# A recurrence-plus-MLP kernel: raw rooms without clears, first queries' values in quarter tiles, one masked copy on ScalarE, one reversal on VectorE

## The chip, the cores and the metric

The kernel runs on one core of one Trainium2 chip. The metric is the device time of one launch in microseconds, as the median of several runs. A core has five instruction queues that the text names as the profile does: PE (TensorE, with PEld for its weight loads), DVE (VectorE), ACT (ScalarE), POOL (GpSimd) and SP (SyncE, which here issues nearly all DMAs). Each executes its own instructions in the order in which the program issues them.

## The reference

Two blocks follow one another. The first is a gated linear recurrence for 4 batches and 8 heads over 768 tokens with head size 48; the second is a two-layer MLP with SiLU on the 3072 x 384 rows that come out.

```python
for t in range(S):                       # S = 768, D = 48
    cur = einsum('bhd,bhe->bhde', u[None] * kt, vt)
    y[:, :, t] = einsum('bhd,bhde->bhe', rt, state + cur)
    state = wt[:, :, :, None] * state + einsum('bhd,bhe->bhde', kt, vt)
x = y.transpose(0, 2, 1, 3).reshape(3072, 384)
h = x @ w_in                             # 384 x 2048
out = (h * (1 / (1 + exp(-h)))) @ w_out  # 2048 x 384
```

All inputs and outputs are 32-bit floats.

## The kernel before

**Units.** The work is cut into 12 units: 6 chunks of 128 tokens (`L`) times 2 pairs of batches (`NB = 2`). A unit holds 16 head-batches; 8 heads are 4 pairs `p` of an even and an odd head `e`, at partition rows 0 to 47 and 64 to 111. The second batch of a pair is kept in reversed token order.

**Scores by levels.** Within a unit the decayed products of queries and keys are made in 7 levels (`NL`), level `l` with blocks of `c = 2^l` tokens. `scores(i, l)` (L725) has PE make the products, and `keep_masked` (L719, its copy is L722) has DVE write them with a mask into the tile `score[128 keys, e, 8 (batch, pair), 128 queries]`. Levels in the tuple `COPIED` (L686) are written by plain ACT copies instead (L741). Level 6 writes only the second half of the queries (columns 64 to 127). The diagonal, the bonus with `u`, is written by `bonus_write` (L601, its copy L604), two DVE copies over the whole score. Between the levels POOL grows the keys (`grow_keys`, L645), ACT moves odd keys (L615) and DVE grows the queries (L627).

**Values.** `y(i, b)` (L873) multiplies values and scores for units 0 and 1: 4 pairs times 2 heads, each a matmul of 128 keys x 64 value columns against 128 queries (L879), and one ACT copy to `yt` (L883). `dense_x` (L911) packs the rows for the MLP, `up` makes 256 hidden columns with SiLU, `down` the second product.

**Loading.** Units 0 and 1 (`NTOK = 2`) load tokens of r, k, w into rooms `raw` (two slots, three rooms of 128 x 1024 each; a room's first 768 columns hold tokens and PE transposes them, reading up to 16 columns further). `twos` (L99) also names the 16 columns behind the tokens, and L264 clears them with one DVE memset for each of the six rooms, at the very start. Units from 2 on write the same rooms by blocks of 32 tokens (L123), which fill only 16 of 32 columns for half of the partitions; so `clear(i)` (L406, its ACT copy L401, 128 x 1536) zeroes these columns once for either slot. The values of batch 2 are loaded in one piece for units 0 and 1 (L138) and turned round by `reverse_v` (L410): a matmul with a mirror matrix (L414) and an ACT copy (L415). From unit 2 on they are loaded as four blocks of 32 rows (L143), and DVE turns each block (L417, a stream shuffle).

**Order.** The order is written out by hand with `do(...)`. For unit 0 the six levels run with other work between them (`others`), then y(0), `dense_x`, the first `up`; then the levels of unit 1 with `up` of unit 0; then y(1). Beside this the 16 pieces of the MLP's weights are rounded one after the other: `head_weight` (ACT L223, L225), `tail_weight` (ACT L231, writes the PSUM tile `p_w`), `join_weight` (DVE L242 and L243, reads it), `add_weight` (POOL L255). `p_w` has one buffer, and unit 0's diagonal stands in it before `bonus_write(0)` has read it. At the start DVE makes masks (L327 to L353) from counters that POOL writes into the score's memory; only then may POOL clear the score (L355), and after it POOL makes the first product of unit 0's bonus (L448).

Of the kernel before, what the change touches and what calls it, by code (L numbers as in the profile page):

```python
# [8 lines left out]
F32 = mybir.dt.float32  # L9
# [29 lines left out]
def kernel(  # L39
# [11 lines left out]
    nc = tc.nc  # L51

    B, H, S, D = r.shape
    DM, DF = moe_w_in.shape
    L = 128
    NL = 7
    NB = 2
    NP = H // 2
    PD = 64
# [7 lines left out]
    NSLOT = 2  # L67
    NTOK = 2
# [8 lines left out]
    ps = ctx.enter_context(tc.tile_pool(name="ps", bufs=1, space=bass.MemoryType.PSUM))  # L77
# [6 lines left out]
    def bank(name, *dims):  # L84

        have = banks[name][turns_of[name] % 2][:]
        turns_of[name] += 1
        steps, n = [], 1
        for d in dims[::-1]:
            steps.insert(0, [n, d])  # L90
            n *= d
        return bass.AP(tensor=have.tensor, offset=have.offset, ap=[have.ap[0], *steps])


    raw = const.tile([128, NSLOT, 3, NB, H, PD], F32, name="raw")
    WRK = {"w": 0, "r": 1, "k": 2}
    vt, vq, whole = {}, {}, {}

    def twos(room):  # L99

        flat = room.rearrange("p b h d -> p (b h d)")
        return flat[:, 0:H * 2 * D].rearrange("p (h s) -> p h s", h=H), flat[:, H * 2 * D:H * 2 * D + PD - D]

    def load_twos(to, src, i, queues):
        n, b0 = units[i]
# [4 lines left out]
    def load_tokens(i):  # L110
        for name, src in (("k", k), ("r", r), ("w", w)):
            load_twos(twos(raw[:, i % NSLOT, WRK[name]])[0], src, i, [nc.sync, nc.scalar if i == 0 else nc.sync])
# [13 lines left out]
    def load_values(i):  # L126
        n, b0 = units[i]
        t0 = n * L

        rooms = [pin.tile([128, H * D + PD - D], F32, name=name, bufs=2) for name in ("vt", "vq")]  # L130
        if n == 0:
            for room in rooms:
                nc.vector.memset(room[:, H * D:], 0.0)
        whole[i] = rooms
        vt[i], vq[i] = (room[:, 0:H * D].rearrange("p (h d) -> p h d", h=H) for room in rooms)
        nc.sync.dma_start(out=vt[i], in_=v[b0, :, t0:t0 + L, :].rearrange("h t d -> t h d"))
        if i < NTOK:
            nc.sync.dma_start(out=vq[i], in_=v[b0 + 1, :, t0:t0 + L, :].rearrange("h t d -> t h d"))  # L138
            return

        for g in range(4):
            t1 = t0 + L - (g + 1) * 32
            nc.sync.dma_start(out=vq[i][g * 32:(g + 1) * 32], in_=v[b0 + 1, :, t1:t1 + 32, :].rearrange("h t d -> t h d"))  # L143
# [114 lines left out]
    zero = const.tile([128, 1], F32, name="zero")  # L258
# [3 lines left out]
    for i in range(NTOK):  # L262
        for x in range(3):
            nc.vector.memset(twos(raw[:, i, x])[1], 0.0)  # L264
# [13 lines left out]
    load_tokens(1)  # L278
    load_weight(1)
    load_values(0)  # L280
    for i in due[-1][2:]:
        load_weight(i)
    load_values(1)

    ident = const.tile([128, 128], F32, name="ident")
# [5 lines left out]
    room = pt.tile([128, 4, DM // 2], F32, name="partial", bufs=1).rearrange("p x d -> p (x d)")  # L291
# [41 lines left out]
    NSC = 1  # L333
    score = const.tile([128, NSC, 2, Q, L], F32, name="score")
# [62 lines left out]
            to = t.rearrange("p (b q) (i s) -> p q b i s", b=NB, s=2)[:, :, :, :, s]  # L397
            nc.scalar.copy(out=to, in_=p_tr)

    def clear_all(room):  # L400
        nc.scalar.copy(out=room, in_=zero[:, :, None].to_broadcast(list(room.shape)))  # L401

    def clear_state():
        nc.gpsimd.memset(state, 0.0)

    def clear(i):  # L406

        clear_all(raw[:, i % NSLOT].rearrange("p x b h d -> p (x b h d)").rearrange("p (g d) -> p g d", d=32)[:, :, D - 32:32])

    def reverse_v(i):  # L410
        flat = vq[i].rearrange("p h d -> p (h d)")
        if i < NTOK:
            p_v = bank("p_m", H * D)
            nc.tensor.matmul(p_v, lhsT=mirror, rhs=flat, start=True, stop=True)  # L414
            nc.scalar.copy(out=flat, in_=p_v)  # L415
            return
        nc.vector.stream_shuffle(out=flat, in_=flat, mask=list(range(31, -1, -1)))  # L417
# [53 lines left out]
    at = 768  # L471
# [211 lines left out]

        return x % 2, x if x % 2 == 0 else (L >> l) - 1 - x

    COPIED = (0, 5, 0), (0, 6, 0), (1, 6, 0)  # L686

    def score_products(i, l, queries, sc):
        c, ni = 1 << l, L >> (l + 1)
# [35 lines left out]
    def scores(i, l, *between):  # L725
# [8 lines left out]
        def keep(e):  # L734
            if (i, l, e) in COPIED:

                for b in range(NB):
                    for x in range(ni):
                        first = 2 * x * c if b == 0 else L - (2 * x + 1) * c
                        rows, columns = slice(first, first + c), slice((2 * x + 1) * c, (2 * x + 2) * c)  # L740
                        nc.scalar.copy(out=score[rows, i % NSC, e, b * NP:(b + 1) * NP, columns],  # L741
                                       in_=sc[e][rows, b * NP:(b + 1) * NP, x * c:(x + 1) * c])
                return
            keep_masked(i, l, e, sc)
# [85 lines left out]
    p_yt, p_kv, yt = {}, {}, {}  # L830
# [28 lines left out]
    def y_values(i, e):  # L859
# [9 lines left out]
        for x in range(2):  # L869
            nc.scalar.copy(out=yt[i][PD * e:PD * e + D, x::2, :, :],  # L870
                           in_=p_yt[i, e][PD * x:PD * x + D].rearrange("p (q b) t -> p q b t", b=NB))

    def y(i, b):  # L873

        p_yt[i, b] = ps.tile([128, NP, L], F32, name="p_h", bufs=2) if i == 0 else bank("p_m", NP, L)
        for p in range(NP):
            for e in range(2):
                h = 2 * p + e
                nc.tensor.matmul(p_yt[i, b][PD * e:PD * e + PD, p, :], lhsT=whole[i][b][:, h * D:h * D + PD],  # L879
                                 rhs=score[:, i % NSC, e, b * NP + p, :], start=(p == 0), stop=(p == NP - 1))  # L880
        if b == 0:
            yt[i] = pt.tile([128, NP, NB, L], F32, name="yt", bufs=1)
        nc.scalar.copy(out=yt[i][:, :, b, :], in_=p_yt[i, b])  # L883
# [49 lines left out]
    def both(fn, i, *args):  # L933
        return [(fn, i, b, *args) for b in range(NB)]

    def block_loads(i, names="wkr"):
        return [(load_blocks, i, name, g) for name in names for g in range(4)]

    def mix(i):
# [43 lines left out]
        if i + 1 < len(units):  # L983
            loads.insert(len(loads) // 2, (load_values, i + 1))
# [109 lines left out]
    def do(*steps):  # L1094
        for fn, *args in steps:
            fn(*args)
# [7 lines left out]
    def back(fn, i, *args):  # L1104
# [6 lines left out]
       (make_dense,), (beat, 16))  # L1111

    blocks = block_loads(2)
    others = {1: [(clear, 0), (beat, 6)], 2: [(turn, 1, 0, "r"), (head_weight, 0), (beat, 2)],
              3: [(turn, 1, 1, "r"), (head_weight, 1), (beat, 2)], 4: [(turn, 1, 1, "w"), (reverse_v, 0)],
              5: [(bonus_spread, 0), (bonus_write, 0), (turn, 1, 0, "w")], 6: [*both(turn_in, 1, "k"), *blocks[0:4], (tail_weight, 0)]}
    for l in range(1, NL):
        do((scores, 0, l), *[(grow_keys, 0, l + 1)] * (l + 1 < NL), *others[l])

    do((bonus, 1, 0), (bonus, 1, 1), (bonus, 1, 2), *both(y, 0), (turn_apart, 0), (join_weight, 0), (add_weight,),  # L1120
       (product, 1, 0), (tail_weight, 1), (turn, 1, 0, "k"), (join_weight, 1), (dense_x, 0, 0), (turn, 1, 1, "k"),
       (dense_x, 0, 1), (grow_queries, 1, 0), (odd_ones, 1), (tail_weight, 2), (turn_k, 0), (head_weight, 2),
       (start_keys, 1, nc.gpsimd, True), (add_weight,), (up, 0, 0), (join_weight, 2), *blocks[4:8],
# [3 lines left out]


    others = {1: [(bonus_sum, 1, 0), (bonus_sum, 1, 1), (load_rk, 2), *blocks[8:12]], 2: [*both(update, 0)],
              3: [(bonus_spread, 1), (reverse_v, 1), (clear, 1), (load_values, 2)]}  # L1130

    def piece(i):

# [2 lines left out]
    for m in range(1, 4):  # L1136
        do((piece, m + 3), (scores, 1, m + 1), (grow_keys, 1, m + 2), (up, 0, m + 2), *others[m])
    do((head_weight, 8), (join_weight, 7), (scores, 1, 5), (grow_keys, 1, 6), (add_weight,), (tail_weight, 8), (up, 0, 6),
       (bonus_write, 1))

    do((scores, 1, NL - 1), (bonus, 2, 0), (bonus, 2, 1), (join_weight, 8), (add_weight,), (bonus_sum, 2, 0), (bonus, 2, 2), (up, 0, 7), *both(y, 1), (turn_apart, 1),
       (tail_weight, 9), (turn_k, 1), (dense_x, 1, 0), (head_weight, 9, [0]), (dense_x, 1, 1), (head_weight, 9, [1]),
       (join_weight, 9), (add_weight,), (tail_weight, 10), (head_weight, 10), *both(update, 1), (bonus_sum, 2, 1), (load_rk, 3), (up, 1, 0), *both(turn, 2, "w"))
    blocks = block_loads(3)

    others = {0: [(up, 1, 1), (down, 0, 0, 0), *both(turn, 2, "k"), (product, 2, 0), (product, 2, 1)],
              1: [(up, 1, 2), *both(turn, 2, "r"), *[(product, 2, l) for l in range(2, NL)], *blocks[0:3]],
              2: [(down, 0, 0, 1), (odd_ones, 2), (start_keys, 2, nc.gpsimd, True), (grow_queries, 2, 0), *blocks[3:6]],
              3: [(up, 1, 3), (start_keys, 2, nc.gpsimd, False), (reverse_v, 2), *blocks[6:9]], 4: [(level, 2, 1), (up, 1, 4), *blocks[9:12]],
              5: [(down, 0, 0, 2), (up, 1, 5), (weight_sums, 0)]}  # L1150
# [15 lines left out]
    for i in range(3, len(units)):  # L1166
# [4 lines left out]
        room = (1, 1, 0, 2, 1, 1, 1, 1, 1, 2, 2, 1, 1) if i < NPAIR else (2, 1, 2, 2, 1, 1, 1, 2, 1, 1, 1)  # L1171
# [37 lines left out]
```

## Time and profile before

| what | value |
|---|---|
| median of 4 runs | 601.8 us (601.66, 601.74, 601.85, 604.5) |
| the profiled execution | 600.91 us, of which the span of the core's instructions is 599.1 us |
| busy in the span | PE 590.7, PEld 529.9, DVE 417.9, POOL 361.4, ACT 232.9 us |
| granted TensorE clock | 1.0 in every slice |
| two ACT clears of raw rooms (L401) | 1.47 us each, at 16.06 and 60.01 |
| two reversals by mirror (L414, L415) | PE 0.9 us and ACT 0.48 us each, at 22.96 and 58.67 |
| y(0), y(1) (L879) | PE from 29.34 and from 66.57 to the next work at 31.71 and 68.47 |
| six memsets of 128 x 16 (L264) | 0.21 us together, 72 ns each, at 0.87 |

A line of the timeline has the start in us from the span's beginning, the length in us, engine, line, operation, output and input tiles, shapes and count; in brackets stands how long the engine was idle before it and what ended that. Several instructions of one kind in a row are merged to one line. In the chain of waits the work is followed back from the last instruction to what released it. An idle time of an engine that the end doesn't hang on costs nothing. The span's first 64 us are units 0 and 1, in which five queues wait for one another; behind them PE works nearly without a gap to the end.

### The profile page before, as it was taken

To read this page: it belongs to the slowest core of one execution; us is meant where nothing else is said; L and a number is where in the kernel's file an instruction comes from. 1 tells how busy PE (TensorE), PEld (TensorE's weight loads), DVE (VectorE), ACT (ScalarE), POOL (GpSimd) and SP (SyncE) were. 2 spreads that over 40 slices of the span, in tenths; PEclk is the share of its full clock that TensorE was granted. 3 is DMA by queue.
4 is the path that set the end of the run, shared out by engine and by line. 5 is a ranking of instruction groups with operands and counts; after the bars stand their busy time and mean duration, and the time that the engine had idled before them with its cause. 6 is when DMAs were issued, how large, how long until landed. Compare 5 with 4: busy or idle time off the path is not lost.

```text
span 599.1 us, 15465 instructions
## 1 busy us (share of the span) xinstructions
PE 590.7 (99%) x6142; PEld 529.9 (88%) x6142; DVE 417.9 (70%) x709; ACT 232.9 (39%) x516; POOL 361.4 (60%) x414
## 2 busy tenths in 40 slices
PE   8999999999999999999999999999999999999997
PEld 7787876799899899899899899889889889889997
DVE  7879788798696695596696696687587587542041
ACT  6788884431530530540450351361351251250110
POOL 6998778357678668378478478577467558500000
PEclk9999999999999999999999999999999999999999
DMA  9966693343542543642632743633553531101000
GB/s 225 294 143 188 135 309 47 55 79 49 130 63 57 110 65 54 135 62 51 139 59 52 139 61 55 133 59 53 109 84 51 121 55 27 36 2 28 27 1 26
DMA packets 203080, 53.45 MB, mean 89 GB/s; under 512 B 186752, under 2 KB 194816, under 8 KB 203008
## 3 DMA queue, kind: packets, MB, share of 16 engines
q1 hardware_dynamic: 201424, 51.88, 42.3%
q8 instruction: 48, 0.79, 0.6%
q10 hardware_dynamic: 1584, 0.59, 0.5%
q14 instruction: 24, 0.20, 0.1%
HBM read 43.21 MB, written 5.24 MB: 81 GB/s over the span
## 4 chain that ended last, share of the span: by engine, by line
PE 80%; DVE 6%; SPq 3%; DMA 3%; POOL 3%; issue 2%; ACT 2%; DVEq 0%; POOLq 0%; ACTq 0%
PE p_h L1001 35%; PE p_o L1067 31%; PE p_m L1023 3%; PE p_sc L704 2%; PE p_m L865 2%; SPq L123 2%; PE p_m L844 2%; PE p_m L704 2%; DVE score L722 1%; POOL tk L645 1%; DMA tokens_w<-in_w_dram 1%; PE p_sc L820 1%; DMA raw<-in_r_dram 1%; SPq L143 1%; PE p_sc L893 1%
## 5 line engine op out<-in xcount | busy, mean ns | idle before, releaser
L1001 PE MATMUL p_h<-xt,w_in_sb 128*128 128x256 f32 x1152 | 259.4, 382 | 0.8 <-POOL tk L669 0.7
L1001 PEld LDWEIGHTS p_h<-xt,w_in_sb 128*128 128x128 f32 x1152 | 215.7, 190 | 31.8 <-POOL tk L669 0.9
L1010 ACT ACTIVATE gt<-p_h 128x512 f32<-128x512 f32 x90 | 53.6, 596 | 175.1 <-PE p_h L1001 174.8
L645 POOL TENSOR_TENSOR tk<-tk,tw 128x256 f32<-128x256 f32 x128 | 94.3, 758 | 33.1 <-issue 20.8
L1067 PE MATMUL p_o<-own,temps 128*128 128x192 f32 x528 | 88.7, 327 | 0.4 <-DVE temps L1076 0.2
L1067 PEld LDWEIGHTS p_o<-own,temps 128*128 128x128 f32 x528 | 86.0, 190 | 1.3 <-DVE temps L1076 1.3
L507 POOL TENSOR_TENSOR ruk<-tokens_rk 128x768 f32<-128x768 f32 (+1 forms) x32 | 50.7, 1595 | 60.3 <-DMA tokens_rk<-in_k_dram 35.6
L1067 PE MATMUL p_o<-w_out_sb,gt 128*128 128x192 f32 x508 | 86.6, 327 | 0.0
L1067 PEld LDWEIGHTS p_o<-w_out_sb,gt 128*128 128x128 f32 x508 | 83.3, 190 | 1.0 <-DVE partial L1076 0.4
L1049 DVE TENSOR_TENSOR temps<-gt 128x256 f32<-128x256 f32 x84 | 58.0, 691 | 25.6 <-ACT gt L1010 25.4
L627 DVE TENSOR_TENSOR tr<-tr,tw 128x512 f32<-128x512 f32 x61 | 53.9, 883 | 17.8 <-PE p_m L704 14.1
L422 POOL TENSOR_TENSOR tw<-tw 128x256 f32<-128x256 f32 (+6 forms) x83 | 41.1, 495 | 35.1 <-DVE tw L374 31.2
L615 ACT COPY tk<-tk 128x256 f32<-128x256 f32 x52 | 21.0, 403 | 105.2 <-POOL tk L645 77.3
L722 DVE COPY_PREDICATED score<-mask,p_sc 128x512 f32<-128x512 int8 x42 | 31.2, 798 | 3.4 <-PE p_sc L704 3.2
L1049 DVE TENSOR_TENSOR temps<-temps,gt 128x256 f32<-128x256 f32 x43 | 30.7, 715 | 1.5
L1067 PE MATMUL p_o<-w_out_sb,temps 128*128 128x192 f32 x176 | 30.4, 326 | 0.0
L541 DVE TENSOR_REDUCE block_sums<-ruk 128x4 f32<-128x192 f32 (+1 forms) x48 | 24.2, 545 | 7.1 <-POOL ruk L507 7.1
L1067 PEld LDWEIGHTS p_o<-w_out_sb,temps 128*128 128x128 f32 x176 | 28.9, 190 | 0.0
L1076 DVE TENSOR_TENSOR partial<-p_o,partial 128x192 f32<-128x192 f32 x33 | 11.7, 355 | 24.4 <-PE p_o L1067 24.4
L870 ACT COPY yt<-p_m 48x512 f32<-48x512 f32 x40 | 23.2, 581 | 13.8 <-PE p_m L865 13.1
L1076 DVE TENSOR_TENSOR temps<-p_o,partial 128x192 f32<-128x192 f32 x22 | 7.8, 357 | 29.6 <-PE p_o L1067 23.3
L704 PEld LDWEIGHTS p_sc<-tr,tk 48*32 48x32 f32 (+1 forms) x1312 | 18.3, 119 | 11.2 <-issue 8.1
(188 smaller groups left out, 823.0 us busy)
## 6 DMA issues: line engine op xcount, KB each, us to landing
w_out_sb<-in_moe_w_in_dram SPq DMA_DIRECT2D x6, 768.0 KB, 7.7
w_out_sb<-in_moe_w_out_dram SPq DMA_DIRECT2D x4, 768.0 KB, 5.4
own<-in_moe_w_out_dram SPq DMA_DIRECT2D x4, 768.0 KB, 5.7
tokens_rk<-in_r_dram SPq DMA_DIRECT2D x8, 384.0 KB, 4.4
tokens_rk<-in_k_dram SPq DMA_DIRECT2D x8, 384.0 KB, 5.3
tokens_w<-in_w_dram SPq DMA_DIRECT2D x8, 384.0 KB, 6.3
xt<-yt SPq DMA_DIRECT2D x60, 48.0 KB, 1.9
raw<-in_w_dram SPq DMA_DIRECT2D x80, 32.0 KB, 2.1
```

The lines of the kernel that those rows point to most:

```text
L422: engine.tensor_tensor(out=up, in0=t[:, :, 0::2], in1=t[:, :, 1::2], op=ALU.mult)
L507: mul = lambda out, one, two: nc.gpsimd.tensor_tensor(out=out, in0=one, in1=two, op=ALU.mult)
L541: add = lambda out, have: nc.vector.tensor_reduce(out=out, in_=have, axis=mybir.AxisListType.X, op=ALU.add)
L627: nc.vector.tensor_tensor(out=odd, in0=odd, in1=tw[i][l][:, :, 0::2][:, :, :, None].to_broadcast([128, Q, L >> (l + 1), c]), op=ALU.mult)
L645: nc.gpsimd.tensor_tensor(out=out, in0=have, in1=odd_products(i, l, b, *blocks), op=ALU.mult)
L704: nc.tensor.matmul(to, lhsT=tk[i][rows, X[l % 2] + p, x * m:(x + 1) * m], rhs=have, start=True, stop=True)
L722: nc.vector.copy_predicated(out=dst, mask=masks[l][:, :, None].to_broadcast([128, NB, NP, ni, c]), data=sc[e].rearrange("p (b q) (i c) -> ...
L870: nc.scalar.copy(out=yt[i][PD * e:PD * e + D, x::2, :, :], in_=p_yt[i, e][PD * x:PD * x + D].rearrange("p (q b) t -> p q b t", b=NB))
L1001: nc.tensor.matmul(p_h[:, a, :], lhsT=w_in_sb[:, c, f * 128:(f + 1) * 128], rhs=xt[i][:, c, :], start=(c == 0), stop=(c == KC - 1))
L1010: nc.scalar.activation(out=gt[i, m], in_=p_h, func=AF.Silu)
L1049: nc.vector.tensor_tensor(out=out, in0=one, in1=two, op=op)
L1067: nc.tensor.matmul(p, lhsT=left(f), rhs=right[:, f, :], start=(f == 0), stop=(f == FH - 1))
```

## The change

Only the first two units are touched.

- `twos` names all 256 columns behind a room's tokens instead of 16, so the six memsets of L264 are 128 x 256. `clear` and `clear_all` are gone: what the blocks of units 2 and 3 leave unwritten holds old tokens, in rows that no result reads.
- Unit 1's batch-2 values are loaded in four blocks of 32 rows, as from unit 2 on, and turned by DVE. The step moves from beside level 4 of unit 1 to just ahead of `bonus_write(1)`. Unit 0 keeps the mirror.
- `COPIED` gains (0, 6, 1): the last level of unit 0 is written by ACT for the odd heads too.
- A new step `y_first` stands ahead of y(0) and y(1). For the first 64 queries only 64 keys count (rows 0 to 63 of batch 1, rows 64 to 127 of the reversed batch 2); it makes 16 matmuls of 64 x 64 weights against 64 queries, which use quarters of PE's array. `y` keeps the second 64 queries: 16 matmuls of 128 x 64 weights against 64 queries. Both PSUM tiles are taken at the beginning of `y_first`.

```diff
@@ twos
-        return flat[:, 0:H * 2 * D].rearrange(...), flat[:, H * 2 * D:H * 2 * D + PD - D]
+        return flat[:, 0:H * 2 * D].rearrange(...), flat[:, H * 2 * D:]
@@ load_values
-        if i < NTOK:
+        if i == 0:
             nc.sync.dma_start(out=vq[i], in_=v[b0 + 1, :, t0:t0 + L, :].rearrange("h t d -> t h d"))
             return
@@ clear_all and clear are taken out; reverse_v
-        if i < NTOK:
+        if i == 0:
@@
-    COPIED = (0, 5, 0), (0, 6, 0), (1, 6, 0)
+    COPIED = (0, 5, 0), (0, 6, 0), (0, 6, 1), (1, 6, 0)
@@
+    def y_first(i):
+
+        half = L // 2
+        for b in range(NB):
+            p_yt[i, b] = ps.tile([128, NP, L], F32, name="p_h", bufs=2) if i == 0 else bank("p_m", NP, L)
+        for p in range(NP):
+            for e in range(2):
+                for b in range(NB):
+                    at, rows = (2 * p + e) * D, slice(b * half, (b + 1) * half)
+                    nc.tensor.matmul(p_yt[i, b][PD * e:PD * e + PD, p, 0:half], lhsT=whole[i][b][rows, at:at + PD],
+                                     rhs=score[rows, i % NSC, e, b * NP + p, 0:half], start=(p == 0), stop=False)
+
     def y(i, b):
 
-        p_yt[i, b] = ps.tile([128, NP, L], F32, name="p_h", bufs=2) if i == 0 else bank("p_m", NP, L)
+        half = L // 2
         for p in range(NP):
             for e in range(2):
                 h = 2 * p + e
-                nc.tensor.matmul(p_yt[i, b][PD * e:PD * e + PD, p, :], lhsT=whole[i][b][:, h * D:h * D + PD],
-                                 rhs=score[:, i % NSC, e, b * NP + p, :], start=(p == 0), stop=(p == NP - 1))
+                nc.tensor.matmul(p_yt[i, b][PD * e:PD * e + PD, p, half:], lhsT=whole[i][b][:, h * D:h * D + PD],
+                                 rhs=score[:, i % NSC, e, b * NP + p, half:], start=False, stop=(p == NP - 1))
@@ the order
-    others = {1: [(clear, 0), (beat, 6)], ...
+    others = {1: [(beat, 6)], ...
-    do((bonus, 1, 0), (bonus, 1, 1), (bonus, 1, 2), *both(y, 0), ...
+    do((bonus, 1, 0), (bonus, 1, 1), (bonus, 1, 2), (y_first, 0), *both(y, 0), ...
-              3: [(bonus_spread, 1), (reverse_v, 1), (clear, 1), (load_values, 2)]}
+              3: [(bonus_spread, 1), (load_values, 2)]}
-       (bonus_write, 1))
+       (reverse_v, 1), (bonus_write, 1))
-    do((scores, 1, NL - 1), ..., (up, 0, 7), *both(y, 1), ...
+    do((scores, 1, NL - 1), ..., (up, 0, 7), (y_first, 1), *both(y, 1), ...
```

## The prediction

> **What bounds the kernel now.** I read the busy times first, then the chain of waits, then the timeline where the chain passes the edited steps.
>
> ```profile
> PE 590.7 (99%) x6142; PEld 529.9 (88%) x6142; DVE 417.9 (70%) x709; ACT 232.9 (39%) x516; POOL 361.4 (60%) x414
> PE 80%; DVE 6%; SPq 3%; DMA 3%; POOL 3%; issue 2%; ACT 2%; DVEq 0%; POOLq 0%; ACTq 0%
> ```
>
> PE is the bound, but it is 80% of the chain and not 99%: the chain in order of time shows that up to `up(0,7)` at 63.78 us it runs through POOL, DVE and ACT, and through PE alone nearly everywhere behind. So a microsecond counts in two ways. Up to 63.78 only what delays `up(0,7)` counts; after it, only PE's own work does. The whole change lies ahead of 73 us.
>
> **The start: wider memsets.** These rows, from the timeline's first 16 us, are one row of dominoes.
>
> ```profile
> 0.87 0.21 DVE L264 MEMSET raw<- 128x16 f32 x6
> ...
> 1.51 0.62 DVE L327 TENSOR_SCALAR temps<-tok_all 128x2 int32<-128x2 int32 x7 [0.31 <-POOL tok_all L325]
> ...
> 5.47 0.09 DVE L432 MEMSET own_sums<- 128x32 f32 x1
> 5.65 1.81 POOL L355 MEMSET score<- 128x2048 f32 x1 [1.86 <-DVE own_sums L432]
> ...
> 7.57 1.20 POOL L448 TENSOR_TENSOR tokens_rk<-raw 128x384 f32<-128x384 f32 x1
> 8.80 0.55 DVE L457 TENSOR_REDUCE own_sums<-tokens_rk 128x8 f32<-128x384 f32 x1 [0.91 <-POOL tokens_rk L448]
> ```
>
> The six memsets stand ahead of DVE's masks; POOL's clear of the score waits 1.86 us for these; the bonus product L448 follows on POOL, and DVE waits 0.91 us for it. From L457 on the chain is tight. The six grow from 16 to 256 columns. DVE memsets of this trace: 59 ns for 1 column, 72 for 16, 85 for 32, so some 0.83 ns a column, and 72 + 240 x 0.83 = 271 ns for 256. Narrow ones start every 28 ns, 44 less than they last; with the same overlap the wide ones start every 227 ns, and six cost 6 x (227 - 28) = 1.19 us more; without overlap 6 x 271 - 170 = 1.46. Of this 0.31 is hidden, since L327 waits that long for POOL anyway, and 0.21 more, since one mask (its start comes 0.38 after the last one's, others 0.165) waits for POOL's counters, which will be long done. Left are 0.67 to 0.94. L448 takes 1.20 here with a DVE product beside it until 7.90, and 1.01 in both later rows of its form; moved behind that product it should win 0.19 back. That gives +0.48 to +0.75; I take **+0.6**. Bounds: 0, if a wide memset costs what a narrow one does, and +0.94.
>
> The Trainium skill, "VectorE: DVE Perf Modes", section "Zero memsets can be issued as uint32 (trn2)", says that a memset takes one cycle per element whatever the type. That speaks against this part: by the page's 0.96 GHz it is an estimate of 1.04 ns a column, six intervals of some 0.27 us, and about +0.8 in place of +0.6.
>
> **Unit 0: a clear gone, a copy moved, y(0) split.** These lines are from the timeline between 16 and 36 us.
>
> ```profile
> 16.06 1.47 ACT L401 COPY raw<-zero 128x1536 f32<-128x1536 f32 x1
> ...
> 17.70 0.41 ACT L615 COPY tk<-tk 128x256 f32<-128x256 f32 x1 [0.18 <-POOL tk L645]
> ...
> 22.34 5.78 SPq L138 DMA_DIRECT2D vq<-in_v_dram  x1
> ...
> 26.40 2.52 DVE L604 COPY_PREDICATED score<-own_mask,p_w 128x1024 f32<-128x1024 int8 x2
> ...
> 27.80 0.76 ACT L741 COPY score<-p_sc 64x256 f32<-64x256 f32 x2
> ...
> 28.96 0.89 ACT L231 ACTIVATE p_w<-w_out_sb 128x768 f32<-128x768 uint16 x1 [0.40 <-DVE score L604]
> 29.03 0.74 DVE L722 COPY_PREDICATED score<-mask,p_sc 128x512 f32<-128x512 int8 x1
> ...
> 29.82 0.74 PEld L879 LDWEIGHTS p_h<-score,vt 128*64 128x64 f32 x13 [0.34 <-DVE score L722]
> 29.89 0.96 DVE L242 SCALAR_TENSOR_TENSOR p_w<-w_out_sb,p_w 128x768 uint32<-128x768 uint32 x1
> ...
> 32.30 0.89 ACT L231 ACTIVATE p_w<-w_out_sb 128x768 f32<-128x768 uint16 x1
> ```
>
> *The clear* (1.47 us) ends at 17.53, and ACT then still waits 0.18 us for POOL: POOL is the cover, and taking the clear out gives **0**.
>
> *The copy.* Today DVE writes the odd heads from 29.03 to 29.77. In its place ACT makes two more copies, 0.76 us like those at 27.80. They write where `bonus_write` writes, so they wait for its second copy (26.40 + 2.52 = 28.92) and end near 29.73. For y(0) that is no gain (29.77 before). Behind them in ACT's queue stands `tail_weight(0)`, the L231 at 28.96: it moves 0.75 later, ends at 30.6, and DVE's L242 and L243, which today follow at 29.89, end at 32.55 in place of 31.83. `tail_weight(1)` needs `p_w` from them: 32.6, not 32.30.
>
> *y(0).* `y_first` can run on PE while ACT copies (score's first half is finished at 28.92, PE's transposes at about 29.3). Only 16 matmuls with 64 queries are left after 29.8. L865 at 122 us has the spacing: 0.107 us for 128 queries, 0.055 for 64. So PE reaches the next step (transposes, now 31.71) at about 30.8: 0.9 early. But the reader of `yt` is `dense_x`, its copy to `xt` stands on ACT behind `tail_weight(1)`, and the other half's copy on DVE behind `join_weight(1)`. Following ACT from 32.6: L394 and L395 until 34.1, L919 at 34.05 (33.98 before), `tail_weight(2)` 35.7 (35.65). Following DVE: L919 at 35.6 (35.32), so `up(0,0)` 0.3 late; by `tail_weight(3)` and DVE's L242 at 40.43 about 0.2 is left. POOL starts 0.75 late at 31.91 and is full until 47.1, but waits 0.57 us there for DVE: again 0.2. I take **+0.2**; bounds -0.9 (all of y's lead arrives) and +0.75 (POOL's delay stays).
>
> *Loads.* Unit 1's reversed values become four issues in place of the single one at 22.34, which took 5.78 us, while the sibling of equal size just before it took 0.53: it waits for room behind the weights, and four quarters wait for the same room. **0**; the upper bound is the second rival below.
>
> **Unit 1: reversal on DVE, a clear gone, y(1) split.** From the timeline between 58 and 80 us:
>
> ```profile
> 61.91 1.83 POOL L255 TENSOR_TENSOR w_in_sb<-temps 128x768 uint32<-128x768 uint32 x1
> ...
> 63.78 2.46 PEld L1001 LDWEIGHTS p_h<-xt,w_in_sb 128*128 128x128 f32 x12 [0.23 <-POOL w_in_sb L255]
> ...
> 65.07 0.74 DVE L722 COPY_PREDICATED score<-mask,p_sc 128x512 f32<-128x512 int8 x1
> ...
> 66.57 1.09 PE L879 MATMUL p_m<-score,vt 128*64 128x128 f32 x16
> ```
>
> `up(0,7)` waits for weights from POOL, which the chain shows busy from 56.6 to 63.74. The mirror matmul (0.9 on PE), its copy (0.48) and the clear (1.47) on ACT were all beside that: **0**. DVE gains a shuffle: ten of this form (128x384) average 580 ns. It stands ahead of `bonus_write(1)`; the level-6 copy at 65.07 then ends at 66.4 in place of 65.81. Its readers, y(1)'s second halves, come behind `y_first` at about 67.2. **0**, with +0.58 if that cover of 0.8 goes. Behind it on DVE, `join_weight(8)` ends at 68.3; ACT's next tail starts at 69.07 today.
>
> y(1) itself is on the chain. Before: 16 x 0.107 = 1.71. After: 16 x 0.055 = 0.88 for the second halves, and the quarters by the score matmuls of almost their shape (48x64 weights, 64 queries): 16 weight loads in 0.56, 0.035 each. At the border between quarter and half tiles at 121.93 the next start comes 0.15 later, 0.1 more than inside. 0.88 + 0.56 + 0.10 = 1.54: **-0.2**. Bounds 0 and -0.3: ACT, full from 69.07, ends the copy that `up(1,0)` at 72.83 needs at 72.56.
>
> The Trainium skill, "TensorEngine Tiling (Array Packing)", section "Key Properties", says that changing the tiling mode drains TensorE. This agrees with the 0.1 us at that border; by the rule alone, with no size given, the gain could only be smaller.
>
> **Sum.** +0.6 + 0 + 0.2 + 0 + 0 - 0.2 = +0.6, against this execution: 600.91 + 0.6 = 601.5. The median shown is 601.8, 0.9 above it; on that scale, on which the prediction is made, **602.4**.
>
> **Rivals.**
> 1. *The start is free and y(0)'s lead arrives.* If memsets cost 0 and ACT's order costs nothing: 0 - 0.9 - 0.2 = -1.1, 600.7. For it: y(0) is on the chain today for 1.96 us. Against it: `tail_weight(0)` stands behind the new copies.
> 2. *SP falls behind: slower.* SP has hardly a gap from 0 to 84 us. If each of the three extra issues holds it like the longest L143 piece (1.25 us; all four took 2.81), it is 3.75 late, and so are the weights that land at 80.15. ACT waits 0.36 for them already, and 0.54 of slack follows at 83.48, with the 0.6 by which all is late anyway: above 1.1 us on SP, PE pays. 3.75 - 1.1 + 0.6 = +3.2: 605.0. Against it: weights 6 and 7 keep more room, and SP's wait looks like one for volume.
> 3. *It doesn't do what it says:* `y_first` waits for level 6 too, if the order is kept per tile and not per column. Then unit 0's PE work starts at 29.8 in one piece, y(0) ends 0.5 later than above, still ahead of 31.71; sum as forecast, 602.4 to 602.9.
>
> **Chances.** Forecast 0.55, rival 1 0.17, rival 2 0.12, rival 3 0.08, and 0.08 for a gain I don't see (0.06 of it over 3 us). Half a percent is 3.0 us, about what a measurement of this kernel can tell from no change. All that I can price as removable from the path (0.9 + 0.3) stays below it; only rival 2 passes it. So faster 0.06, same 0.82, slower 0.12. The range takes the lower bounds (601.8 - 1.2 = 600.6) and above the forecast the bounds of the parts (0.94 + 0.75 + 0.58 = 2.3, 604.1), and half of the way to rival 2 beyond that: 600.6 to 604.6.
>
> **What would show it.** Right: L355 about 0.7 us later than 5.65 and L457 0.6 later than 8.80; the first L231 near 29.7 plus that shift; PE's step after y(0) earlier against `bonus_write(0)`; `up(0,7)` 0.8 after 63.78; y(1) in 1.5 to 1.7 us. Wrong: memset starts every 0.03 us; `up(0,7)` ahead of 63.78; SP's block loads behind 28.30 by over 1 us; new PE gaps after 80 us.

## The result

| | before | after |
|---|---|---|
| median of all runs on the same chips | 601.45 us (72 runs, 600.5 to 604.5) | 602.58 us (47 runs, 601.3 to 606.21) |
| profiled execution | 600.91 us, span 599.1 | 602.32 us, span 600.5 |

The ratio is 1.0019 with a 95% interval of 1.0013 to 1.0025: some 1.1 us slower (0.8 to 1.5), well inside the half percent that counts as no change. The forecast was 602.4.

Lines of the changed kernel are up to 7 lower than before's until L734, and 5 higher from L884 on: L441 is before's L448, L450 is L457, L662 is L669, L697 is L704, L813 is L820, L1006 is L1001; `y_first` is L875.

The page of the changed kernel, busy times and the chain's shares:

```profile
PE 589.2 (98%) x6204; PEld 529.2 (88%) x6204; DVE 417.5 (70%) x710; ACT 229.9 (38%) x515; POOL 363.0 (60%) x414
PE 83%; POOL 4%; DVE 3%; DMA 1%; SPq 1%; ACT 1%; issue 1%; DVEq 0%; POOLq 0%; ACTq 0%
```

PE is 1.5 us less busy and ACT 3.0 less, and the span is 1.4 us longer: what was taken out of the engines' work was not what the time hung on. Where the difference arises is read by following the same instructions through both timelines. The start, timeline of the changed kernel:

```profile
0.92 1.64 DVE L264 MEMSET raw<- 128x256 f32 x6
...
3.23 0.58 DVE L328 CAST temps<-temps 128x14 f32<-128x14 int32 x1
3.26 0.53 POOL L346 MEMSET partial<- 128x512 f32 x1
...
6.75 1.81 POOL L355 MEMSET score<- 128x2048 f32 x1 [2.97 <-DVE own_sums L425]
8.68 1.01 POOL L441 TENSOR_TENSOR tokens_rk<-raw 128x384 f32<-128x384 f32 x1
...
9.72 0.55 DVE L450 TENSOR_REDUCE own_sums<-tokens_rk 128x8 f32<-128x384 f32 x1 [2.04 <-POOL tokens_rk L441]
```

The row of dominoes of the prediction falls later by 1.1 us at the clear of the score (6.75 for 5.65), and by 0.92 at L450 (9.72 for 8.80). Unit 0's end, same timeline:

```profile
29.92 0.76 ACT L734 COPY score<-p_sc 64x256 f32<-64x256 f32 x2 [0.45 <-DVE score L597]
30.34 0.27 PE L875 MATMUL p_h<-score,vt 64*64 64x64 f32 x1
30.58 0.88 ACT L231 ACTIVATE p_w<-w_out_sb 128x768 f32<-128x768 uint16 x1
30.97 0.69 PE L884 MATMUL p_h<-score,vt 128*64 128x64 f32 x16
...
36.95 1.32 PE L1006 MATMUL p_h<-xt,w_in_sb 128*128 128x256 f32 x5 [1.32 <-DVE xt L924]
```

`tail_weight(0)`, the L231, is 1.62 late: the 0.90 that everything is late by here, and 0.72 for the two copies ahead of it at 29.92. PE's transposes behind y(0) come at 32.05; without y's lead these would stand at 31.71 + 0.90 = 32.61, so 0.56 us was won on PE. But `up(0,0)` is at 36.95 for 36.03: 0.92 late, as if nothing had been won. `up(0,7)` is 1.13 late, y(1) takes 1.71 us (67.70 to 69.41) for 1.90, and `up(1,0)` is 0.94 late. Then one more step comes, on ACT and PE:

```profile
82.06 0.97 ACT L223 ACTIVATE temps<-w_out_sb 128x768 bf16<-128x768 bf16 x1 [1.31 <-DMA w_out_sb<-in_moe_w_out_dram]
...
90.48 0.70 PE L697 MATMUL p_sc<-tr,tk 48*64 48x64 f32 x32 [0.93 <-POOL tk L662]
```

The same two lines of before, from its timeline:

```profile
80.18 0.96 ACT L223 ACTIVATE temps<-w_out_sb 128x768 bf16<-128x768 bf16 x1 [0.36 <-DMA w_out_sb<-in_moe_w_out_dram]
...
89.05 0.70 PE L704 MATMUL p_sc<-tr,tk 48*64 48x64 f32 x32 [0.44 <-POOL tk L669]
```

ACT waits 1.31 us instead of 0.36 for the weights of piece 12; from these the work goes through DVE's joins and POOL's L255 to POOL's L662, which stands behind it in POOL's queue, and PE's gap is 0.49 longer. From there to the end the shift stays between 1.2 and 1.8 us.

### The profile page after: what moved, and what is told of

The parts are those of the page before. It is cut to its first block, busy times and chain, and to the rows that moved or that the text cites. A ratio compares the mean times of both kernels' runs of the same rounds, so it can differ in the third digit from the quotient of the medians.

```text
span 600.5 us, 15585 instructions
## 1 busy us (share of the span) xinstructions
PE 589.2 (98%) x6204; PEld 529.2 (88%) x6204; DVE 417.5 (70%) x710; ACT 229.9 (38%) x515; POOL 363.0 (60%) x414
## 4 chain that ended last, share of the span: by engine, by line
PE 83%; POOL 4%; DVE 3%; DMA 1%; SPq 1%; ACT 1%; issue 1%; DVEq 0%; POOLq 0%; ACTq 0%
PE p_h L1006 37%; PE p_o L1072 32%; PE p_m L1028 3%; PE p_sc L697 3%; PE p_m L858 2%; PE p_m L837 2%; POOL w_in_sb L255 2%; PE p_m L697 2%; DMA w_out_sb<-in_moe_w_out_dram 1%; POOL tk L638 1%; PE p_sc L813 1%; PE p_sc L898 1%; SPq L123 1%; POOL tk L662 1%; DVE p_w L242 1%
## 5 line engine op out<-in xcount | busy, mean ns | idle before, releaser
L1006 PE MATMUL p_h<-xt,w_in_sb 128*128 128x256 f32 x1152 | 259.6, 382 | 2.2 <-DVE xt L924 1.3
L1006 PEld LDWEIGHTS p_h<-xt,w_in_sb 128*128 128x128 f32 x1152 | 215.6, 190 | 33.6 <-POOL tw L415 1.5
L620 DVE TENSOR_TENSOR tr<-tr,tw 128x512 f32<-128x512 f32 x61 | 58.6, 961 | 18.0 <-PE p_m L697 14.4
L1054 DVE TENSOR_TENSOR temps<-gt 128x256 f32<-128x256 f32 x84 | 51.6, 614 | 25.6 <-ACT gt L1015 25.3
L697 PEld LDWEIGHTS p_sc<-tr,tk 48*32 48x32 f32 (+1 forms) x1312 | 18.2, 119 | 11.3 <-issue 7.5
```

Of the source, the lines that this page charges most:

```text
L620: nc.vector.tensor_tensor(out=odd, in0=odd, in1=tw[i][l][:, :, 0::2][:, :, :, None].to_broadcast([128, Q, L >> (l + 1), c]), op=ALU.mult)
L697: nc.tensor.matmul(to, lhsT=tk[i][rows, X[l % 2] + p, x * m:(x + 1) * m], rhs=have, start=True, stop=True)
L1006: nc.tensor.matmul(p_h[:, a, :], lhsT=w_in_sb[:, c, f * 128:(f + 1) * 128], rhs=xt[i][:, c, :], start=(c == 0), stop=(c == KC - 1))
L1054: nc.vector.tensor_tensor(out=out, in0=one, in1=two, op=op)
```

## The experiments

All twelve were timed beside the kernel before. This table has what the readings below rest on: by how many us an instruction starts later than in before's profile. "Units 0 and 1" is `up(1,0)` less `start_keys` of unit 0 (11.18 in before), so it leaves out the start with its memsets and what the arrival of the first loads varies by. "Weight 12" is the L223 at 80.18, so the time at which ACT uses the weight; in e2 and e5 it had landed earlier, at 78.93 and 78.68, before ACT came to it. "PE at 89.69" is the matmul behind the step shown above.

| run | start_keys | up(1,0) | units 0 and 1 | weight 12 | PE at 89.69 | ratio of times, 95% interval |
|---|---|---|---|---|---|---|
| after | 0.92 | 0.94 | +0.02 | 1.88 | 1.43 | 1.0019 (1.0013 to 1.0025) |
| e1_late_memset | 0.42 | 0.50 | +0.08 | 0.41 | 0.37 | 1.0023 (1.0002 to 1.0043) |
| e2_wide_memset_alone | 0.92 | 0.92 | 0.00 | 0.45 | 0.92 | 1.0004 (0.9990 to 1.0019) |
| e3_mirror_back | 0.92 | 0.89 | -0.03 | 2.08 | 1.60 | 1.0013 (0.9995 to 1.0031) |
| e4_quarters_alone | -0.01 | -0.69 | -0.68 | 0.41 | -0.09 | 1.0022 (1.0005 to 1.0040) |
| e5_copy_alone | 0.66 | 0.79 | +0.13 | 0.32 | 0.74 | 1.0002 (0.9993 to 1.0010) |
| e6_copy_and_quarters | 0.88 | 0.89 | +0.01 | 1.59 | 1.13 | 1.0023 (1.0009 to 1.0037) |
| e7_four_loads_alone | 0.34 | 0.28 | -0.06 | 0.74 | 0.28 | 1.0013 (1.0003 to 1.0024) |
| e8_late_and_mirror | 0.11 | 0.06 | -0.05 | 2.16 | 1.64 | 1.0032 (1.0018 to 1.0047) |
| e12_before_again | 0.07 | 0.03 | -0.04 | 0.45 | -0.04 | 1.0001 (0.9990 to 1.0011) |

The times of e1, e4, e6, e7, e8 and e9 to e11 all came out above what was expected of them; the places below are what the expectations can be held against.

**The memsets.** Two runs bracket them: only these added to before (e2), and in the changed kernel only 16 columns at the start, the other 240 behind `own_sums`, which POOL's clear of the score waits for (e1).

```diff
 # e2, on the kernel before
-        return flat[:, 0:H * 2 * D].rearrange("p (h s) -> p h s", h=H), flat[:, H * 2 * D:H * 2 * D + PD - D]
+        return flat[:, 0:H * 2 * D].rearrange("p (h s) -> p h s", h=H), flat[:, H * 2 * D:]
 # e1, on the changed kernel
-            nc.vector.memset(twos(raw[:, i, x])[1], 0.0)
+            nc.vector.memset(twos(raw[:, i, x])[1][:, 0:PD - D], 0.0)
...
     nc.vector.memset(own_sums, 0.0)
+    for i in range(NTOK):
+        for x in range(3):
+            nc.vector.memset(twos(raw[:, i, x])[1][:, PD - D:], 0.0)
```

> The kernel before with the wide memsets alone (the clears and all else stay). Theory: the start is the same as with the change, so POOL's clear at 6.75 and up(0,0) at 36.95 in place of 36.03, up(0,7) at 64.7, ratio 1.0015. Rival (the start is only late together with the other edits): up(0,0) within 0.3 us of 36.03, ratio 1.000 to 1.0005.

> The changed kernel, but each of the six rooms is cleared in two steps: 16 columns at the start as before the change, the other 240 behind DVE's masks and its memset of own_sums. Theory (the wide memsets delay the masks, POOL's clear of the score and the first bonus product): POOL's clear starts again near 5.65 us (6.75 with the change), up(0,0) on PE starts 0.9 earlier than with the change, at about 36.05, and the time falls by 0.9 of the 1.13 lost, to a ratio of about 1.0004 against before. Rival (the loss comes from the copy moved to ScalarE and the late join of the weights): up(0,0) stays at 36.9, ratio 1.0019 as with the change.

e2 took 602.47 us against 601.76 (12 runs). Its timeline has the changed kernel's start to 0.02 us (six memsets in 1.64, the cast 0.58, the clear of the score at 6.75). The first reduce, `up(0,0)`, `up(0,7)`, `up(1,0)` and PE at 192 us are all later by 0.91 to 0.92: a pure shift, the memsets' whole price against this one profile of before, that no slack up to there takes up. But before's profile has nearly the earliest start of all. In the other kernels with narrow memsets `start_keys` is up to 0.88 late too, since another row of the start ends last there: in e5 DVE waits for the load of `u` (L452 at 9.92), in e6 `start_keys` itself waits 1.00 us for ACT's copies of `tw`. The mean of the seven such rows of the table is 0.35, so against them the wide memsets cost some 0.6 us, an estimate. e2's time, a ratio of 1.0004, can't tell 0 from 0.92. In e1's timeline the clear of the score is back at its old time:

```profile
2.16 0.35 DVE L328 CAST temps<-temps 128x14 f32<-128x14 int32 x1
...
5.56 1.54 DVE L428 MEMSET raw<- 128x240 f32 x6
5.65 1.81 POOL L355 MEMSET score<- 128x2048 f32 x1 [1.86 <-DVE own_sums L425]
```

Its first reduce is 0.09 late for 0.92, `up(0,0)` 0.46 late for 0.92 (its `start_keys` is 0.42 late in any case), and its profiled execution (600.73 us) is 1.6 us below the changed kernel's. But its median is not: 603.13 us (12 runs, 600.39 to 607.74). The place of the loss in the profile is shown; that moving the memsets gains time is not.

**The split of y and the copy on ACT.** Each alone on the kernel before (e4, e5), and both (e6). The changed kernel's `y_first` and `y` are taken over unaltered.

```diff
 # e5, on the kernel before
-    COPIED = (0, 5, 0), (0, 6, 0), (1, 6, 0)
+    COPIED = (0, 5, 0), (0, 6, 0), (0, 6, 1), (1, 6, 0)
 # e4, on the kernel before: y_first and y as in the change, and
-    do((bonus, 1, 0), (bonus, 1, 1), (bonus, 1, 2), *both(y, 0), ...
+    do((bonus, 1, 0), (bonus, 1, 1), (bonus, 1, 2), (y_first, 0), *both(y, 0), ...
...
-    do((scores, 1, NL - 1), ... (up, 0, 7), *both(y, 1), ...
+    do((scores, 1, NL - 1), ... (up, 0, 7), (y_first, 1), *both(y, 1), ...
 # e6: both
```

> The kernel before with only the values split (y_first ahead of y(0) and y(1)). Theory: y(1) takes 1.7 in place of 1.9 us on PE, y(0) is released by DVE's copy as before and ends 0.5 to 0.9 earlier, of which ScalarE and DVE pass on little, since weight work stands between; up(0,0) 0 to 0.3 earlier, the next matmuls after y(1) 0.2 to 0.5 earlier in all, ratio 0.9992 to 0.9997. Rival (y(0) sets the path until up(0,0)): 0.9 at up(0,0), ratio 0.998.

> The kernel before with only the last level of unit 0 for odd heads written by ScalarE. Theory: ScalarE's copies wait for bonus_write's second copy and end when VectorE's single copy ended, so y(0) gains nothing, tail_weight(0) goes back by 0.7 to 29.7 and join_weight(0) to 30.6; up(0,0) is 0.2 to 0.4 later than 36.03, and a fast path through POOL (full from join_weight(0) to 47) carries up to 0.75; ratio 1.0003 to 1.0010. Rival (a freed VectorE is worth more than ScalarE's delay): up(0,0) earlier, ratio below 0.9997.

> The kernel before with the split values and the copy moved to ScalarE together. Theory: the first queries' matmuls run while ScalarE copies, so y(0)'s end is 0.9 earlier than before, but tail_weight(0) is 0.7 late; the two cancel at up(0,0) (within 0.2 of 36.03), and y(1) gives 0.2: ratio 0.9995 to 1.0000. Rival (the two help each other): up(0,0) 0.5 or more earlier, ratio 0.999 or below.

e4 took 602.62 against 601.76 us, e5 601.54 and e6 603.07 against 601.53 (11 to 12 runs each). The column "units 0 and 1" shows how the two edits meet: the split alone -0.68, the copy alone +0.13, both +0.01. So the copy costs 0.1 where y is in one piece and 0.7 where it is split. The five kernels with both lie between -0.05 and +0.08. Two more runs that are told below have the split without the copy: e11 with -0.72, and e9 with only -0.22, where the lead of 0.55 at `up(0,0)` is gone at `up(0,7)` already (-0.03). So e4's lead is no constant either. Why the copy costs more with the split, stands in two timelines. e4, with the copy on DVE:

```profile
29.05 0.75 DVE L722 COPY_PREDICATED score<-mask,p_sc 128x512 f32<-128x512 int8 x1
...
30.09 0.69 PE L891 MATMUL p_h<-score,vt 128*64 128x64 f32 x16
...
31.17 0.70 PE L820 MATMUL p_sc<-ident,tk 48*128 48x48 f32 x16
...
35.48 1.32 PE L1013 MATMUL p_h<-xt,w_in_sb 128*128 128x256 f32 x5 [0.74 <-POOL tk L669]
```

and e5, with the copy on ACT:

```profile
31.24 0.96 DVE L242 SCALAR_TENSOR_TENSOR p_w<-w_out_sb,p_w 128x768 uint32<-128x768 uint32 x1 [1.67 <-ACT p_w L231]
...
36.72 0.45 PE L1001 MATMUL p_h<-xt,w_in_sb 128*128 128x256 f32 x1 [1.18 <-DVE xt L919]
```

With the split alone PE is at the transposes 0.54 us earlier (31.17 for 31.71), and so is `up(0,0)` (35.48 for 36.03), which waits for POOL as it did before. With the copy the row of tail (L231), join (L242) and DVE's half of `dense_x` (L919) is 0.7 late against the rest, and `up(0,0)` now waits for that DVE copy, in e5 as in the changed kernel. In before this row had some slack, since `up(0,0)` waited 0.74 us for POOL and not for it. The copy uses it up: alone it costs little, but with it the row of DVE is the one that ends last, and y's lead ends in a wait.

e4 also shows what becomes of a lead that does reach `up(1,0)`. Its timeline at the step of 90 us:

```profile
88.96 0.70 PE L704 MATMUL p_sc<-tr,tk 48*64 48x64 f32 x32 [1.04 <-POOL tk L669]
89.01 0.91 ACT L223 ACTIVATE temps<-own 128x768 bf16<-128x768 bf16 x1 [2.00 <-DMA own<-in_moe_w_out_dram]
```

PE arrives 0.69 early and waits 1.04 us in place of 0.44: 0.60 of it is given back in one place, since the weights came no sooner (weight 12 at +0.41).

**The loads in four pieces.** By the second rival, SP's extra issues delay the weights. Taken back in the changed kernel, together with DVE's reversal (e3); taken back with the late memsets too (e8); and put alone into the kernel before, four pieces in natural order with the mirror kept (e7).

```diff
 # e3, on the changed kernel; e8: this and e1's edit
-        if i == 0:
+        if i < NTOK:
             nc.sync.dma_start(out=vq[i], in_=v[b0 + 1, :, t0:t0 + L, :].rearrange("h t d -> t h d"))
...
-              3: [(bonus_spread, 1), (load_values, 2)]}
+              3: [(bonus_spread, 1), (reverse_v, 1), (load_values, 2)]}
...
-       (reverse_v, 1), (bonus_write, 1))
+       (bonus_write, 1))
 # e7, on the kernel before
-            nc.sync.dma_start(out=vq[i], in_=v[b0 + 1, :, t0:t0 + L, :].rearrange("h t d -> t h d"))
+            for g in range(4 if i == 1 else 1):
+                n_rows = 32 if i == 1 else L
+                nc.sync.dma_start(out=vq[i][g * n_rows:(g + 1) * n_rows],
+                                  in_=v[b0 + 1, :, t0 + g * n_rows:t0 + (g + 1) * n_rows, :].rearrange("h t d -> t h d"))
```

> The changed kernel, but unit 1's reversed values are loaded by one DMA and turned by the mirror matmul and the ScalarE copy, at their old place. Theory (four issues hold SP 1.6 us longer, the weights that ScalarE's head_weight(12) waits for land at 82.04 in place of 80.15, and PE loses 0.49 us between 81 and 90): up(0,7) as with the change (64.9, or 0.1 earlier), unit 2's first score matmuls 0.5 earlier than 90.48, ratio 1.0011. Rival (the later landing has nothing to do with the four issues): the step between 81 and 90 stays, ratio 1.0019 or above.

> The kernel before, but unit 1's batch-2 values are loaded in four pieces of 32 rows, in their old order; the mirror still turns them. Theory: SP is through with them about 1 to 1.6 us after 28.12, the block loads behind start as much later, some of it is left at 75 us, and PE loses up to 0.5 us between 81 and 90: ratio 1.0004 to 1.0009. Rival: SP's wait is for room alone, the four are through at 28.1 to 28.4, ratio within 0.0003 of 1.

> The changed kernel with both repairs: 240 of the 256 columns cleared behind the masks, and unit 1's values by one DMA and the mirror. What is left of the change: no clears, the split values, the copy on ScalarE. Theory: up(0,7) at 63.8, y(1) 0.2 shorter, no step at 81 to 90; 0.2 to 0.4 faster than before, ratio 0.9993 to 0.9998. Rival (some other part of the change costs): ratio above 1.0003.

e3 took 602.77 against 601.76 us (12 runs), e7 602.05 and e8 603.29 against 601.53 (12 and 8 runs). I had come to think, from the longer waits for weight 12, that the four issues were behind the step at 90 us. That falls. e3 has the single load and the step all the same, and weight 12 even later:

```profile
82.25 0.93 ACT L223 ACTIVATE temps<-w_out_sb 128x768 bf16<-128x768 bf16 x1 [1.55 <-DMA w_out_sb<-in_moe_w_out_dram]
```

PE's gap behind it is 1.14 us. e8 has the single load too, is back at +0.06 at `up(1,0)`, and still has the step (+1.64). e7 has the four issues and no step (+0.28 at both places). On SP itself the changed kernel's four issues took 8.15 us, from 21.65 to 29.80, where before's single one took 5.78, and the block loads followed at 29.94 for 28.30. Later the changed kernel's SP catches up: it issues weight 12 at 75.84, 0.27 after before's 75.57, but the DMA ends at 82.04 for 80.15. There most of the delay is in the transfer. It isn't so in every kernel: e3 issues weight 12 by 1.17 late and e8 by 2.02, both without the four issues, and in e8 that is nearly all of the delay. What e7's time says is another matter: its interval, 1.0003 to 1.0024, leaves open that the four issues cost something elsewhere.

**Unit 2's value loads moved.** These stand ahead of weight 12 on SP. Moved behind `join_weight(9)`, weight 12 should land sooner: on e4 (e9), on before (e10), and with all parts that had looked good by their profiles: the split, no clears, late memsets, the copy back on DVE and the mirror (e11).

```diff
 # e9, e10, e11
-              3: [(bonus_spread, 1), (reverse_v, 1), (clear, 1), (load_values, 2)]}
+              3: [(bonus_spread, 1), (reverse_v, 1), (clear, 1)]}
...
-       (join_weight, 9), (add_weight,), ...
+       (join_weight, 9), (load_values, 2), (add_weight,), ...
```

> The split values alone, and unit 2's values are loaded behind join_weight(9), so that SP issues weights 12 and 13 first. Theory (the split wins 0.7 us until up(1,0), and PE gives it back at 89, where it waits by way of POOL and ScalarE for weights 12 to 14, the last that SP brings): weight 12 is issued 3 us earlier and has landed when ScalarE comes to it, PE's wait at 89 (1.04 in the split alone, 0.44 before) falls to 0.4 or less, and the lead of 0.7 is still there behind 114 us: ratio 0.998 to 0.9995. Rival (the loss of kernels with the split is not in these loads): the wait at 89 goes but the time stays at the 1.0022 of the split alone.

> The kernel before with only that load moved: the reference for the last run. Theory: PE's wait of 0.44 at 89 shrinks by up to 0.3, nothing else changes: ratio 0.9993 to 1.0000. Rival (the move in itself is worth what the split with it shows): the same ratio as the split with the load moved.

> What the runs so far speak for, together: the split values, no clears, only 16 columns cleared at the start and 240 behind the masks, the copy of unit 0's last level back on VectorE, unit 1's values by one DMA and the mirror, and unit 2's values loaded behind join_weight(9). Theory: POOL's clear of the score at 5.65 as before, up(0,0) 0.5 earlier than 36.03 (unless the first tokens of w land late in the profiled execution), up(1,0) 0.7 earlier, and the lead is kept: ratio 0.998 to 0.9995. Rival (kernels with the split run slower for another reason): ratio above 1.001.

All three lost, against 601.6: e9 605.97 us (ratio 1.0077, 1.0053 to 1.0101), e10 606.17 (1.0064, 1.0040 to 1.0089), e11 606.61 (1.0077, 1.0059 to 1.0094), six runs each. In e10 weight 12 is used as early as in before (-0.04, for +0.45 in the unchanged e12), but weight 14 is issued 1.7 us later (84.81 for 83.11) and its use is 3.86 late. e10's timeline:

```profile
92.02 0.91 ACT L223 ACTIVATE temps<-own 128x768 bf16<-128x768 bf16 x1 [4.34 <-DMA own<-in_moe_w_out_dram]
...
100.61 0.69 PE L704 MATMUL p_sc<-tr,tk 48*64 48x64 f32 x32 [2.48 <-POOL tk L645]
```

One wait is taken away and a longer one comes two pieces later. And it costs more than its gap; that is told in the last section.

**The kernel before once more.** With no edit, to learn what two profiles of one kernel differ by.

> The kernel before itself, unchanged, as a measure of how far two runs of one program lie apart, in time and in the profile. Expected: ratio within 0.0005 of 1, PE's starts within 0.9 us of the first profile (the start waits for tokens from memory, and these differ from execution to execution). If kernels with the split owe their spread to chance, this one shows a like share of runs above 603.

601.89 against 601.6 us (12 runs). Up to 78 us the instructions of PE, ACT and DVE start within 0.1 us of the other profile's. SP's issues differ by up to 1.55 us all the same, and four of POOL's instructions by up to 0.87. Weight 12 comes 0.45 later, and the span is 1.2 us longer (600.3). So a difference of 0.3 us at `up(1,0)` is a finding, while a difference of 1 us at the end of a single profile is none.

## Why the prediction was right, step by step

**The time** was right, 602.4 for 602.58, and so was "no change". But it stood on a median of 601.8 for before, where 72 runs give 601.45. The change itself was forecast as +0.6 and is +1.1 (0.8 to 1.5): the sum is too small by some 0.5. The two misses have opposite signs, so that the figure came within 0.2 is luck. "No change" is not: the terms that the profiles confirm are all far below half a percent.

**The memsets: right in mechanism, mis-sized.** +0.6 was forecast, +0.92 measured at the first reduce, in the changed kernel and in e2 alike, near the upper bound of 0.94. Two terms were off. One wide memset lasts 272 ns, for 271 forecast, but the six start 0.265 us apart (0.92 to 2.51 for the six), not 0.227: the overlap of narrow memsets doesn't carry over to wide ones. And the wait of a mask for POOL's counters did go, but the small cast L328 took 0.58 us for 0.35, in the changed kernel, e2 and e3 alike; in all three POOL's memset of `partial` (3.26 to 3.79) runs beside it, which in before it doesn't. That this is the cause was not tested. L441 did fall from 1.20 to 1.01, as forecast. The estimate after the Trainium skill, "VectorE: DVE Perf Modes", section "Zero memsets can be issued as uint32 (trn2)", one cycle per element and some 0.27 us for 256 columns, agrees with the 0.265 measured; it was the better of the two prices. Against the mean start of kernels with narrow memsets, some 0.6 us as worked out above, the forecast of +0.6 would be right, but for another reason than its own: it knew one start only, and no other row that can end last there.

**The clears: right.** ACT's wait for POOL at the next step is 1.54 us for 0.18 (at 18.61): the removed 1.47 turned into idle time. This is read from the profile; no run takes the clears out alone.

**The copy: right.** `tail_weight(0)` was forecast 0.75 later and is 0.72 later; of that 0.02 reaches `up(0,0)` and 0.2 `up(0,7)`, for +0.2 forecast. The lead of y(0) on PE is 0.56, not 0.9: the second halves begin 0.29 us after DVE's copy ends (e4: 29.80 and 30.09) and take 1.08 us, not 0.88. It didn't matter, because by the prediction's own reason the lead doesn't arrive.

**The loads, and unit 1's reversal: right on the path.** Three more issues and a shuffle on DVE at 63.02 (0.59 us) move `up(1,0)` by nothing (e3: -0.03 against +0.02). The level-6 copy ends at 66.82, 1.5 us ahead of y(1)'s second halves at 68.33.

**y(1): right.** -0.2 forecast, -0.19 measured. Both sides of the difference were too low by some 0.18 (1.71 and 1.54 forecast, 1.90 and 1.71 measured). The border between quarter and half tiles is there: starts 0.15 apart, as at 121.93 in before.

**The sum at `up(1,0)`,** in the one pair of profiles: 0.92 + 0.02 = +0.94 for +0.6 forecast; the difference is the memsets.

**What the prediction missed** is the step from 0.94 to 1.43 us at 90 us. Two of its signs of being wrong came: SP's block loads are 1.64 us behind 28.30, and PE waits longer after 80 us. The place is that of rival 2, weight 12, but rival 2's mechanism is not at work (e3, e7). The table's columns suggest a rule for the place: PE at 89.69 is late by `up(1,0)`'s shift or by weight 12's less 0.47, whichever is larger; fitted to these ten runs it holds within 0.13, while e9 and e11 miss it by 0.2. For the changed kernel that is 1.88 - 0.47 = 1.41, for e4 0.41 - 0.47 = -0.06.

**The rivals.** Rival 1 (a free start, y's lead arrives) is refuted by both halves of it: e2's 0.92, and e6's +0.01. Rival 2 loses its mechanism at the step of 90 us, as told; a cost of the four issues elsewhere was not excluded. Rival 3 (`y_first` waits for level 6) is refuted: `y_first` starts at 30.34, ACT's copies end at 30.68.

**What stays open.** *Why weight 12 lands late.* Of the five kernels with both split and copy, four have it at +1.59 to +2.16 and one, e1, at +0.41; the five others at +0.32 to +0.74. No edit explains that, and a profile is one execution. In the unchanged e12, too, SP's issues are up to 1.55 us off before's.

*Which edit the medians charge.* The intervals are 1 to 2.5 us wide, as large as the terms, but they don't point at the memsets. The six kernels with the split stand at 1.0013 to 1.0032, the four others of the table at 1.0001 to 1.0013. The split alone (e4) has 1.0022, with an interval above 1, the wide memsets alone (e2) 1.0004, and e1 and e8, in which the memsets are out of the way, are no faster than the changed kernel. So the memsets' cost, which the profiles show, is not shown to be what the 1.1 us of the medians consist of. By the times it may well be the split, which the prediction put at -0.2 for y(1) and at nothing for y(0). Then the near agreement of +0.6 is luck as well.

*Why kernels with the split scatter more:* 16 of 47 runs of the changed kernel and 28 of 56 of e1, e3, e4, e6 and e8 lie above 603 us, but of before only 4 of 72 beside the changed kernel and 6 of 83 beside the experiments, and of e2, e5, e7 and e12 4 of 47. This may hold a good part of the 1.1 us, and e1's high median with its low profile.

Where the time goes, the traces show in part, since those of e3 (604.0 us), e6 (604.1) and e8 (603.75) are of such executions. From `up(1,0)` to 250 us PE falls behind before's by another 2.2, 2.3 and 3.4 us there: from 85 to 104 us, between 155 and 185 us, and in e6 and e8 at 242 us, where PE waits 0.78 and 0.98 us for the DMA of `xt`. These places are not the split's own: e2 (603.03 us) waits 1.53 us at 242, and the unchanged e12 loses 0.6 us between 155 and 185 and 0.5 at 242. Some of the longest executions lose clock, too: the two longest of the changed kernel, of e1, of e4 and of before beside the experiments and the longest of e7 and e8 have a mean granted clock of 0.994 to 0.997, against 0.999 or 1.0 in all the others of these kernels. The last section shows what such a loss looks like. Why kernels with the split meet these waits more often was not found. No kernel tried beats the one before.

## What to carry to other kernels

In this kernel, bound by PE at 98%, 3 us of work taken off ACT were worth nothing by themselves. Two edits that are each read off one profile need not add up: a lead counts only as far as the slower of the rows that meet there, here -0.68 and +0.13 together +0.01. What is put at the head of a program can go through the whole of it unreduced, as the memsets' 0.92 us do in e2 up to 192 us; but it counts only as far as no other row of the start is late. A profile that confirms a term does not show that the median pays it: here the times point at the split, and the profiles at the memsets. Before a step is read from late in a profile, take a second profile of the same kernel: here PE's work differed by 1.2 us at the end and by 0.1 up to 78 us.

## What the runs showed of the hardware

A short idle time of PE cost more than itself. The windows of e10 have, behind the times, each engine's busy time, then the granted clock, the DMA share and GB/s:

```profile
100.00:104.00 4.00, 3.39 (x38) 2.14 (x39) 3.90 (x4) 0.41 (x1) 2.58 (x2) 0.76 0.41 49
104.00:108.00 4.00, 4.00 (x11) 2.22 (x11) 2.82 (x4) 0.59 (x2) 3.92 (x4) 0.81 0.43 51
108.00:112.00 4.00, 4.00 (x50) 2.46 (x50) 2.37 (x6) 0.60 (x2) 0.91 (x3) 1.00 0.41 48
```

PE idles 2.48 us up to 100.61, and the two windows that follow have a clock of 0.76 and 0.81. They lose 4 x 0.24 + 4 x 0.19 = 1.7 us; with the gap of 2.48 and the 0.42 from earlier that is 4.6, and PE at 114.6 is 4.66 late. e9 shows the same behind a gap of 2.02 us at 97.94, and e11 behind one of 2.49 at 102.01: in windows of 1 us its clock is 1.00 up to 102 and then 0.51, 0.50, 0.50 and 0.79, which again loses 1.7 us. e10's second gap, 1.82 us at 245.58, is followed by 0.68 and 0.89. But e11's first gap, 2.10 us at 96.66, leaves the clock at 1.00, and so do a gap of 1.53 us in e2, at 241.68, and all gaps of before and of the changed kernel behind 74 us, all under 1 us. The Trainium skill, "TensorE: Matmul & The Clock Gate", section "Why this matters for your kernels", warns of idle gaps above about 3 us; here four gaps between 1.82 and 2.49 us were followed by such a loss, and one of 2.10 us was not. What decides between them was not found.
